# A long convolution's spectrum of half 0, stored with one frequency word per row instead of one signal per row

## The chip, the cores and the metric

The kernel runs on one core of a Trainium2 chip. The metric is the device time of one execution, in microseconds (us). Before the change the median of three runs is 1404.55 us (1404.37 to 1404.98). The core has five engines that matter here: PE (matrix multiplications, with the loading of weights counted apart as PEld), DVE and ACT (element-wise work, both read PSUM), POOL (element-wise work in SBUF) and SP, which issues most DMAs.

## The reference

The program is a long convolution, whose result goes through two expert layers. The convolution is the part that the change touches.

```python
def _attn_ref(x, v, pos_emb, w1, w2):          # S = 12480, D = 128
    h_mlp = np.maximum(pos_emb @ w1, 0.0) @ w2
    window = np.exp(-0.01 * np.arange(S))[:, None]
    h_filt = h_mlp * window
    u = x * v
    Uf = np.fft.rfft(u, n=2 * S, axis=1)
    Hf = np.fft.rfft(h_filt, n=2 * S, axis=0)
    y = np.fft.irfft(Uf * Hf[None], n=2 * S, axis=1)[:, :S, :]
    return x * y

def _moe_ref(x, w_in, w_out):    return np.maximum(x @ w_in, 0.0) ** 2 @ w_out
def _moe2_ref(x, w_in, w_out, alpha):
    h = x @ w_in
    return (np.maximum(h, 0.0) + alpha * np.minimum(h, 0.0)) @ w_out
```

## The kernel before

The transform of length L = 110 x 229 = 25190 is done by two small matrix transforms, over NA = 110 and over NB = 229 points, of which symmetry leaves HB = 115 rows and KA = 56 columns, as real and imaginary part K2 = 112 words. All of it is fp32 matmuls; each such matmul stands in the trace as two records of PE and two weight loads. The 128 signals (channels) are worked in two halves of 64, and each has an even and an odd part, so a half's spectrum is 115 partitions x 128 signal parts x 112 words.

Half 0's spectrum lies in gaps of the large tile `G`, which is looked at as HX = 116 rows of two blocks of 128 words (`gap`, L129): a row is one signal part, 112 adjacent words; the first XF = 16 rows are in block 0, the other 112 in block 1 (`U`, L131). Because of the two places, `parts(0)` (L138) names two ranges, of 16 and of 112 rows, and each operation on all of half 0 is issued once for each. Half 1's spectrum lies in one piece in `R2`. The other rows of block 0 serve as staging tiles for the loaded `x` and `v` (`xv_ring`, NV = 10 pairs) and for copies (`a_ring`, `t_ring`).

The work around the change is in stages, written as generators; `run` (L452) interleaves the steps of two of them in program order, by a fixed share. Each engine takes its own instructions in that order.

- `u_stage(0)` (L327) beside `r_stage` (L236): for 16 groups of four signals, `u_mm_a3` does the first transform (L283, L286, L287) and `u_mm_b3` the second (L296, ACT's copy L298, and DVE's sum and difference L301, which write half 0's spectrum). `r_stage` transforms the filter (L242, L244, L248, L249) and spills it. `prep` (POOL, L271 and L210) and `load` (SP, L263) run some groups ahead.
- `u_stage(1)` (L309 to L325, no split) beside `p_stage(0)` (L342): 14 steps n, each in two half steps of four matmuls (L368, the filter's values into a PSUM bank `H`), a DVE product of spectrum and filter (L373) into `T` or the PSUM tile `wide`, then two DVE operations (L382) and the closing sum and difference back into the spectrum (`finish`, L352, on POOL).
- `p_stage(1)`, called `q0`, beside `b_stage(0)` (L386), the inverse transform of half 0: three half steps of `q0` first, then 25 half steps beside 16 steps of `b_stage`. A step has 8 matmuls (L391), each with one signal part's 112 words as weights, and two ACT copies (L399).
- `b_stage(1)` with the decoding of expert weights, then `y_stage` (L444, L445), whose weights are words two apart, and then the two expert layers (L605 to L658), from about 340 us to the end.

Of the kernel before, what the change touches and what calls it, by code (L numbers as in the profile page):

```python
# [9 lines left out]
F32 = mybir.dt.float32  # L10
# [5 lines left out]
ALU = mybir.AluOpType  # L16

S, D, F, FF = 12480, 128, 64, 2048
# [3 lines left out]
KA = HA + 1  # L22
K2 = 2 * KA
HB = (NB + 1) // 2
# [1 line left out]
HX = 2 * HP  # L26
HZ = (HB + 1) // 2
KP = KA // 2
XF = 16
NAP = -(-NA // 16) * 16  # L30
DH = D // 2
DG = 4
NG = DH // DG
# [20 lines left out]
def ring_of(pool, n, shape, dtype, name):  # L54
    return Ring(pool.tile(shape, dtype, name=f"{name}{i}") for i in range(n))
# [3 lines left out]
def kernel(  # L59
# [22 lines left out]
    nc = tc.nc  # L82
# [16 lines left out]
    r_any, r_a, r_b, r_h = Ring(banks), Ring(banks[0:2]), Ring(banks[2:5]), Ring(banks[5:8])  # L99
    r_ab, r_y = Ring([]), Ring([])  # L100

    def bank(ring, p, *dims):
        n = 1
        for d in dims:
            n *= d
        names = "uvwxyz"[:len(dims)]
        return ring()[:p, :n].rearrange(
            f"p ({' '.join(names)}) -> p {' '.join(names)}", **dict(zip(names, dims))
        )
# [3 lines left out]
    R2 = p_r2.tile([128, K2 * 128], F32, name="R2")  # L113
# [8 lines left out]
    isinb, icosb = dfb[:, 1], dfb[:, 2]  # L122
# [5 lines left out]
    gv = G[:K2].rearrange("p (t e x r) -> p t e x r", t=HP, e=2, r=2)  # L128
    gap = [G.rearrange("p (n h x) -> p n h x", h=2, x=128)[:, :, h] for h in range(2)]  # L129

    def U(h, x0, n):  # L131
        if h:
            return R2[:HB].rearrange("p (x k) -> p x k", k=K2)[:, x0:x0 + n]
        if x0 < XF:
            return gap[0][:HB, x0:x0 + n, 128 - K2:128]
        return gap[1][:HB, x0 - XF:x0 - XF + n, 0:K2]

    def parts(h):  # L138
        return [(0, D)] if h else [(0, XF), (XF, D - XF)]

    NV = 10
    at = [XF]

    def rows(n):
        at[0] += n
        assert at[0] <= HX
        return gap[0][:, at[0] - n:at[0]]

    a_ring = [[rows(DG)[:, :, 0:K2] for _ in range(2)] for _ in range(2)]
    t_ring = [rows(DG)[:, :, 0:K2] if i else gap[1][:, D - XF:D - XF + DG, 0:K2] for i in range(2)]  # L150
    n_old = -(-(HP - at[0]) // DG)
    old = [rows(DG) for _ in range(n_old)]
    n_pos = -(-(GH + HZ * NA - 256 * at[0]) // (256 * DG))
# [2 lines left out]
    xv_ring = new + after + old  # L156
    assert len(xv_ring) == 2 * NV
    xv_ring = list(zip(xv_ring[::2], xv_ring[1::2]))
# [99 lines left out]
    def load(n):  # L258
        while loaded[0] <= min(n, 2 * NG - 1):
            k = loaded[0]  # L260
            assert ready[0] > k - NV
            for t, src in zip(xv_ring[k % NV], (xs, vs)):
# [3 lines left out]
    def prep(n):  # L266
        while ready[0] <= min(n, 2 * NG - 1):
            k = ready[0]
            assert loaded[0] > k
            x, v = (t[:NA, :, 0:HB] for t in xv_ring[k % NV])  # L270
            nc.gpsimd.tensor_tensor(out=v, in0=v, in1=x, op=ALU.mult)  # L271
            signed(nc.gpsimd, x, v, DG)
            ready[0] += 1
# [15 lines left out]
    def u_mm_b3(k):  # L289
        hi, lo = a_t.pop(k)  # L290
        ps = [bank(r_b, HB, 2, DG, KA) for _ in range(2)]
        t = t_ring[k % 2][:HB].rearrange("p d (c k) -> p c d k", c=2)
        for eo in (1, 0):
            th, tl = (tab[:, eo] for tab in df3)
            for i, (w, x) in enumerate(((th, lo), (tl, hi), (th, hi))):
                nc.tensor.matmul(ps[eo], lhsT=w, rhs=x[:, eo], start=i == 0, stop=i == 2)  # L296
            if eo:
                nc.scalar.copy(out=t, in_=ps[1])  # L298
        u = U(0, 2 * DG * k, 2 * DG).rearrange("p (d s) (c k) -> p s c d k", s=2, c=2)
        for s, op in enumerate((ALU.add, ALU.subtract)):  # L300
            nc.vector.tensor_tensor(out=u[:, s], in0=ps[0], in1=t, op=op)  # L301

    def u_mm_a(k):
        q, u = (t[:NA, :, 0:HB] for t in xv_ring[k % NV])
# [5 lines left out]
            nc.scalar.copy(out=a_t[k][s], in_=p)  # L310

    def u_mm_b(k):
        h, g = divmod(k, NG)
        a = a_t.pop(k)
        pe = bank(r_b, HB, DG, 2, KA)
        po = bank(r_b, HB, DG, 2, KA)
        nc.tensor.matmul(po[:, :, 0], lhsT=sinb, rhs=a[0][:, :, 1])
        nc.tensor.matmul(pe[:, :, 0], lhsT=cosb, rhs=a[0][:, :, 0])
        nc.tensor.matmul(po[:, :, 1], lhsT=sinb, rhs=a[1][:, :, 0])
        t = t_ring[k % 2][:HB].rearrange("p d (c k) -> p d c k", c=2)  # L320
        nc.scalar.copy(out=t, in_=po)
        nc.tensor.matmul(pe[:, :, 1], lhsT=cosb, rhs=a[1][:, :, 1])
        u = U(h, 2 * DG * g, 2 * DG).rearrange("p (d s) (c k) -> p d s c k", s=2, c=2)
        for s, op in enumerate((ALU.add, ALU.subtract)):
            nc.vector.tensor_tensor(out=u[:, :, s], in0=pe, in1=t, op=op)  # L325

    def u_stage(h, parts=None):  # L327
        for k in range(h * NG, (h + 1) * NG + 1):
            if k < (h + 1) * NG:
                prep(k + NV - 4)  # L330
                load(k + NV - 1)
                u_mm_a3(k, parts) if parts else u_mm_a(k)
                yield
            if k > h * NG:
                u_mm_b3(k - 1) if parts else u_mm_b(k - 1)
                yield
# [3 lines left out]
    p_order += [(j + nj - 6) % nj for j in range(nj)]  # L340

    def p_stage(h, t_ring, r_ring):  # L342
        def at_j(x0, m, j):
            return U(h, x0, m).rearrange("p x (c k) -> p x c k", c=2)[:, :, :, 4 * j:4 * j + 4]

        def finish(n, j, A):
            eng = nc.vector if n == 2 * nj - 1 else nc.gpsimd
            for x0, m in parts(h):
                y = A[:, x0:x0 + m].rearrange("p (d s) c k -> p d s c k", s=2)
                u = at_j(x0, m, j).rearrange("p (d s) c k -> p d s c k", s=2)  # L350
                for s, op in ((0, ALU.add), (1, ALU.subtract)):
                    eng.tensor_tensor(out=u[:, :, s], in0=y[:, :, 0], in1=y[:, :, 1], op=op)  # L352

        for n in range(h * nj, (h + 1) * nj):
            j = p_order[n]
            m = p_order[min(n + 2, 2 * nj - 1)]
            if m not in r_t:
                del r_t[p_order[n - 1]]
                r_t[m] = r_ring()
                nc.sync.dma_start(out=r_t[m].rearrange("p q c k -> p (q c k)"), in_=spill[m])  # L360
            r = r_t[j]
            A = t_ring()
            B = wide[:HB].rearrange("p (x c k) -> p x c k", k=4, c=2)
            for c, out_c in enumerate((A, B)):
                H = bank(r_h, HB, DH, 2, 2, 2)
                for q in range(2):
                    for s in range(2):
                        nc.tensor.matmul(  # L368
                            H[:, :, s, q], lhsT=r[:, q, 2 * s + c], rhs=w2_sb[:, h * D:(h + 1) * D]
                        )  # L370
                hv = H.rearrange("p d s q r -> p (d s) (q r)")
                for x0, m in parts(h):
                    nc.vector.tensor_tensor(  # L373
                        out=out_c[:, x0:x0 + m],
                        in0=at_j(x0, m, j),
                        in1=hv[:, x0:x0 + m].unsqueeze(2).to_broadcast([HB, m, 2, 4]),
                        op=ALU.mult,
                    )
                if c == 0:
                    yield  # L380
            for c, op in ((0, ALU.subtract), (1, ALU.add)):
                nc.vector.tensor_tensor(out=A[:, :, c], in0=A[:, :, c], in1=B[:, :, 1 - c], op=op)  # L382
            finish(n, j, A)
            yield

    def b_stage(h, alone):  # L386
        for g in range(NG):
            for e in range(2):
                p = bank(r_y if alone else r_ab, K2, DG, HX)
                for d in range(DG):  # L390
                    nc.tensor.matmul(  # L391
                        p[:, d], lhsT=U(h, 2 * (g * DG + d) + e, 1)[:, 0], rhs=icosb if e == 0 else isinb
                    )
                dst = gv[:, :, e, h * DH + g * DG:h * DH + (g + 1) * DG]
                src = p.rearrange("p d (t r) -> p t d r", r=2)
                if alone and e and g == NG - 1:
                    nc.vector.tensor_copy(out=dst, in_=src)
                else:
                    nc.scalar.copy(out=dst, in_=src)  # L399
            yield  # L400
# [171 lines left out]
    n = NCH * NT  # L572
    i = j = 0
# [143 lines left out]
    with tc.manual_schedule():  # L717
        with ExitStack() as st:
            late = st.enter_context(tc.tile_pool(name="late", bufs=1, side="right"))
            w2_sb = late.tile([128, 2 * D], F32, name="w2_sb")  # L720
# [23 lines left out]
            (wide,) = last_two("wide", 1024)  # L744
            r_b.items, r_h.items, r_ab.items = six[2:4], six[4:6], six[0:4]
            big = st.enter_context(tc.tile_pool(name="tt", bufs=1, side="right"))
            tt = ring_of(big, 2, [HB, D, 2, 4], F32, "T")
            p0, q0 = p_stage(0, tt, r_ring), p_stage(1, tt, r_ring)
            run((u_stage(1), 2 * NG), (p0, 2 * nj - 4))
            next(back)  # L750
# [13 lines left out]
        with tc.tile_pool(name="wo", bufs=1) as wo:  # L764
# [5 lines left out]
            for _ in ys:  # L770
                n = min(left, 4)
# [159 lines left out]
```

## Time and profile before

| | us |
|---|---|
| median of three runs | 1404.55 |
| the profiled execution's own time | 1402.77 |
| its span, first to last instruction | 1401.0 |
| PE / PEld busy | 1389.3 / 1205.7 |
| DVE / ACT / POOL busy | 1158.4 / 977.8 / 1006.9 |

The numbers of the trace come from the profiled execution; its own time is 1.8 us below the median. Busy time counts an engine as busy while any of its instructions is under way. PE's records overlap one another (the next begins while the last one drains), so PE looks busy even where it is not at its peak; the distance from one record's start to the next tells its pace. Idle time of an engine that sets nothing costs nothing.

### The profile page before, as it was taken

How to read it: one execution, taken by the hardware profiler on the slowest of the kernel's cores; microseconds unless marked ns; L12 is line 12 of the kernel's file. 1: busy time of each engine (PE TensorE's matmuls, PEld its weight loads, DVE VectorE, ACT ScalarE, POOL GpSimd, SP SyncE). 2: the span in 40 equal slices, each digit the busy share in tenths (PEclk: the TensorE clock that was granted, in tenths of full speed). 3: DMA queues.
4: the chain of work that ended last, by engine and by line, in shares of the span. 5: the costliest groups of instructions: out<-in, count | busy, mean ns of one | idle time of the engine just before them, and what ended most of it. 6: DMA issues, size and time to landing. Idle time of an engine off the chain costs nothing.

```text
span 1401.0 us, 22648 instructions
## 1 busy us (share of the span) xinstructions
PE 1389.3 (99%) x7566; PEld 1205.7 (86%) x7566; DVE 1158.4 (83%) x1824; ACT 977.8 (70%) x1850; POOL 1006.9 (72%) x841
## 2 busy tenths in 40 slices
PE   9999999999999999999999999999999999999998
PEld 9999989998888888888888888888888888888898
DVE  5688899786888888888888888788888878888888
ACT  4454322725988778778777877877787787777777
POOL 4954856446787777877777777777777777777777
PEclk9999999999999999999999999999999999999999
DMA  7565323397000000000000000000000000000000
GB/s 209 173 200 177 94 82 109 105 275 218 24 16 1 8 1 9 8 8 8 9 8 0 9 8 9 8 8 8 8 2 8 8 9 8 9 8 1 8 9 19
DMA packets 59016, 66.20 MB, mean 47 GB/s; under 512 B 6226, under 2 KB 48019, under 8 KB 58771
## 3 DMA queue, kind: packets, MB, share of 16 engines
q1 hardware_dynamic: 57802, 60.62, 14.3%
q0 software_dynamic: 688, 3.93, 0.8%
q8 instruction: 59, 0.97, 0.3%
q14 instruction: 58, 0.48, 0.1%
q10 hardware_dynamic: 409, 0.21, 0.1%
HBM read 47.83 MB, written 16.92 MB: 46 GB/s over the span
## 4 chain that ended last, share of the span: by engine, by line
PE 79%; ACT 1%; POOL 1%; DVE 1%; issue 0%; POOLq 0%; DVEq 0%
PE bank L605 19%; PE bank L607 19%; PE bank L606 19%; PE pair L606 6%; PE pair L607 6%; PE pair L605 6%; PE bank L444 2%; PE bank L445 2%; ACT G L399 1%; POOL g L658 1%; ACT pair L517 0%; ACT w_i L487 0%; DVE pair L477 0%; DVE f_w L481 0%; DVE pair L475 0%
## 5 line engine op out<-in xcount | busy, mean ns | idle before, releaser
L658 POOL TENSOR_TENSOR g<-R,g 128x512 fp32r<-128x512 f32 (+1 forms) x601 | 779.4, 1314 | 253.5 <-ACT g L647 241.3
L640 DVE SCALAR_TENSOR_TENSOR R<-bank,e 128x512 f32<-128x512 f32 (+1 forms) x800 | 530.1, 672 | 137.4 <-POOL g L658 99.8
L647 ACT CAST g<-R 128x512 fp32r<-128x512 f32 (+1 forms) x800 | 469.8, 605 | 77.5 <-DVE R L640 70.0
L625 ACT ACTIVATE e<-bank 128x512 f32<-128x512 f32 (+1 forms) x400 | 235.0, 587 | 106.6 <-PE bank L607 104.6
L630 DVE TENSOR_SCALAR e<-bank,alpha 128x512 f32<-128x512 f32 (+1 forms) x266 | 195.0, 733 | 36.0 <-PE bank L607 34.4
L658 DVE TENSOR_TENSOR g<-R,g 128x512 fp32r<-128x512 f32 (+1 forms) x199 | 184.7, 928 | 0.0
L606 PE MATMUL pair<-g,w_o 128*128 128x512 f32 (+1 forms) x400 | 153.7, 384 | 0.4 <-POOL g L658 0.4
L605 PE MATMUL bank<-x,w_i 128*128 128x512 f32 (+1 forms) x400 | 153.8, 384 | 0.0
L605 PE MATMUL pair<-g,w_o 128*128 128x512 f32 (+1 forms) x400 | 153.6, 384 | 0.0
L606 PE MATMUL bank<-x,w_i 128*128 128x512 f32 (+1 forms) x400 | 153.6, 384 | 0.0
L607 PE MATMUL bank<-x,w_i 128*128 128x512 f32 (+1 forms) x400 | 153.5, 384 | 0.0
L607 PE MATMUL pair<-g,w_o 128*128 128x512 f32 (+1 forms) x400 | 153.5, 384 | 0.0
L605 PE MATMUL bank<-g,w_o0b 128*128 128x512 f32 (+1 forms) x350 | 134.4, 384 | 0.0
L606 PE MATMUL bank<-g,w_o0b 128*128 128x512 f32 (+1 forms) x350 | 134.3, 384 | 0.0
L607 PE MATMUL bank<-g,w_o0b 128*128 128x512 f32 (+1 forms) x350 | 134.3, 384 | 0.0
L627 ACT ACTIVATE e<-bank 128x512 f32<-128x512 f32 (+1 forms) x134 | 78.7, 588 | 33.5 <-PE bank L607 32.9
L628 ACT ACTIVATE e<-e,alpha 128x512 f32<-128x512 f32 (+1 forms) x134 | 95.5, 713 | 4.4
L605 PEld LDWEIGHTS bank<-x,w_i 128*128 128x128 f32 x400 | 75.1, 188 | 15.0 <-DVE R L640 0.9
L606 PEld LDWEIGHTS pair<-g,w_o 128*128 128x128 f32 x400 | 75.2, 188 | 14.8 <-POOL g L658 1.0
L607 PEld LDWEIGHTS bank<-x,w_i 128*128 128x128 f32 x400 | 75.1, 188 | 14.4
L607 PEld LDWEIGHTS pair<-g,w_o 128*128 128x128 f32 x400 | 75.1, 188 | 14.4
L606 PEld LDWEIGHTS bank<-x,w_i 128*128 128x128 f32 x400 | 75.2, 188 | 13.8
(137 smaller groups left out, 2526.0 us busy)
## 6 DMA issues: line engine op xcount, KB each, us to landing
r<-spill SPq DMA_DIRECT2D x22, 460.0 KB, 3.2
G<-in_xs_dram SPq DMA_DIRECT2D x32, 224.0 KB, 3.5
G<-in_vs_dram SPq DMA_DIRECT2D x32, 224.0 KB, 3.5
spill<-r SPq DMA_DIRECT2D x14, 460.0 KB, 3.0
out_dram<-R SPq DMA_DIRECT2D x23, 256.0 KB, 2.0
R<-in_xt_dram SPq DMA_DIRECT2D x27, 218.0 KB, 4.2
s_w<-in_moe_w_in_dram SPq DMA_DIRECT2D x16, 256.0 KB, 3.6
s_w<-in_moe_w_out_dram SPq DMA_DIRECT2D x16, 256.0 KB, 2.7
```

Source lines behind the costliest of these rows:

```text
L444: nc.tensor.matmul(pv, lhsT=le, rhs=re, start=True, stop=False)
L445: nc.tensor.matmul(pv, lhsT=lo, rhs=ro, start=False, stop=True)
L605: nc.tensor.matmul(p, lhsT=wl, rhs=xh, start=first, stop=False)
L606: nc.tensor.matmul(p, lhsT=wh, rhs=xl, start=False, stop=False)
L607: nc.tensor.matmul(p, lhsT=wh, rhs=xh, start=False, stop=last)
L625: nc.scalar.activation(out=r, in_=p, func=ACTF.Relu)
L627: nc.scalar.activation(out=r, in_=p, func=ACTF.Relu, scale=-1.0)
L628: nc.scalar.activation(out=r, in_=r, func=ACTF.Copy, scale=alpha[:, t:t + 1])
L630: nc.vector.tensor_scalar(out=r, in0=p, scalar1=0.0, scalar2=alpha[:, t:t + 1], op0=ALU.min, op1=ALU.mult)
L640: nc.vector.scalar_tensor_tensor(out=g, in0=p, scalar=0.0, in1=r, op0=ALU.max, op1=op)
L647: nc.scalar.copy(out=gh, in_=g)
L658: eng.tensor_tensor(out=gl, in0=g, in1=gh.bitcast(F32), op=ALU.subtract)
```

## The change

Half 0's spectrum moves to block 1 of `G` alone, as 112 rows, one per word (c, k) of the spectrum, each with its 128 signal parts side by side, ordered (s, d): s is even or odd part, d the signal. Rows are 256 words apart. `u_cells` gives the weights of one signal part for `b_stage`. `T`, `wide` and the PSUM bank `H` take the same order for half 0 and keep the old one for half 1. `parts` and with it the second instruction of each pair go away. The 16 rows of block 0 that become free are four more staging tiles: two more pairs, NV = 12.

```diff
-    def U(h, x0, n):
-        if h:
-            return R2[:HB].rearrange("p (x k) -> p x k", k=K2)[:, x0:x0 + n]
-        if x0 < XF:
-            return gap[0][:HB, x0:x0 + n, 128 - K2:128]
-        return gap[1][:HB, x0 - XF:x0 - XF + n, 0:K2]
-
-    def parts(h):
-        return [(0, D)] if h else [(0, XF), (XF, D - XF)]
-
-    NV = 10
-    at = [XF]
+    u0 = gap[1][:HB, :K2].rearrange("p (c k) (s d) -> p c k s d", c=2, s=2)
+    u1 = R2[:HB].rearrange("p (d s c k) -> p d s c k", s=2, c=2, k=KA)
+
+    def u_cells(h, d, e):
+        if h:
+            return u1[:, d, e].rearrange("p c k -> p (c k)")
+        return gap[1][:HB, :K2, e * DH + d]
+
+    NV = 12
+    at = [0]
...
     def u_mm_b3(k):
...
-        u = U(0, 2 * DG * k, 2 * DG).rearrange("p (d s) (c k) -> p s c d k", s=2, c=2)
         for s, op in enumerate((ALU.add, ALU.subtract)):
-            nc.vector.tensor_tensor(out=u[:, s], in0=ps[0], in1=t, op=op)
+            u = u0[:, :, :, s, DG * k:DG * (k + 1)].rearrange("p c k d -> p c d k")
+            nc.vector.tensor_tensor(out=u, in0=ps[0], in1=t, op=op)
...
     def u_stage(h, parts=None):
         for k in range(h * NG, (h + 1) * NG + 1):
             if k < (h + 1) * NG:
-                prep(k + NV - 4)
+                prep(k + NV - 6)
                 load(k + NV - 1)
...
     def p_stage(h, t_ring, r_ring):
+        def shaped(t):
+            if h:
+                return t.rearrange("p (d s c k) -> p c (d s) k", s=2, c=2, k=4)
+            return t.rearrange("p (c k x) -> p c k x", c=2, k=4)
+
+        def at_j(j):
+            k = slice(4 * j, 4 * j + 4)
+            if h:
+                return u1[:, :, :, :, k].rearrange("p d s c k -> p c (d s) k")
+            return u0[:, :, k].rearrange("p c k s d -> p c k (s d)")
...
         def finish(n, j, A):
             eng = nc.vector if n == 2 * nj - 1 else nc.gpsimd
-            for x0, m in parts(h):
-                y = A[:, x0:x0 + m].rearrange("p (d s) c k -> p d s c k", s=2)
-                u = at_j(x0, m, j).rearrange("p (d s) c k -> p d s c k", s=2)
-                for s, op in ((0, ALU.add), (1, ALU.subtract)):
-                    eng.tensor_tensor(out=u[:, :, s], in0=y[:, :, 0], in1=y[:, :, 1], op=op)
+            if h:
+                y, u = A.rearrange("p (d s z) -> p s d z", s=2, z=8), u1[:, :, :, :, 4 * j:4 * j + 4]
+                u = [u[:, :, s] for s in range(2)]
+            else:
+                y = A.rearrange("p (z s d) -> p s z d", s=2, z=8)
+                u = [u0[:, :, 4 * j:4 * j + 4, s] for s in range(2)]
+            for s, op in ((0, ALU.add), (1, ALU.subtract)):
+                eng.tensor_tensor(out=u[s], in0=y[:, 0], in1=y[:, 1], op=op)
...
             for c, out_c in enumerate((A, B)):
-                H = bank(r_h, HB, DH, 2, 2, 2)
+                H = r_h()[:HB].rearrange("p (d s q r) -> p s q d r" if h else "p (q r s d) -> p s q d r", s=2, q=2, r=2)
                 for q in range(2):
                     for s in range(2):
-                        nc.tensor.matmul(
-                            H[:, :, s, q], lhsT=r[:, q, 2 * s + c], rhs=w2_sb[:, h * D:(h + 1) * D]
-                        )
-                hv = H.rearrange("p d s q r -> p (d s) (q r)")
-                for x0, m in parts(h):
-                    nc.vector.tensor_tensor(
-                        out=out_c[:, x0:x0 + m],
-                        in0=at_j(x0, m, j),
-                        in1=hv[:, x0:x0 + m].unsqueeze(2).to_broadcast([HB, m, 2, 4]),
-                        op=ALU.mult,
-                    )
+                        nc.tensor.matmul(H[:, s, q], lhsT=r[:, q, 2 * s + c], rhs=w2_sb[:, h * D:(h + 1) * D])
+                hv = H.rearrange("p s q d r -> p (d s) (q r)" if h else "p s q d r -> p (q r) (s d)")
+                o, u = shaped(out_c), at_j(j)
+                if h:
+                    o, u = (x.rearrange("p c x k -> p x c k") for x in (o, u))
+                    hv = hv.unsqueeze(2).to_broadcast([HB, D, 2, 4])
+                else:
+                    hv = hv.unsqueeze(1).to_broadcast([HB, 2, 4, D])
+                nc.vector.tensor_tensor(out=o, in0=u, in1=hv, op=ALU.mult)
...
     def b_stage(h, alone):
...
-                        p[:, d], lhsT=U(h, 2 * (g * DG + d) + e, 1)[:, 0], rhs=icosb if e == 0 else isinb
+                        p[:, d], lhsT=u_cells(h, g * DG + d, e), rhs=icosb if e == 0 else isinb
```

## Rows read from the trace of the kernel before

**Rows 1.** Busy time by stage; columns: stretch, length, engines (x instructions), clock, DMA.
```profile
core 0: us, PE busy (x) PEld busy (x) DVE busy (x) ACT busy (x) POOL busy (x), PEclk, DMA share, GB/s
45.00:116.60 71.60, 71.16 (x586) 68.60 (x585) 58.45 (x122) 35.58 (x77) 44.79 (x39) 1.00 0.64 194
116.60:195.00 78.40, 75.25 (x601) 72.87 (x600) 69.17 (x115) 25.45 (x48) 53.03 (x67) 0.98 0.38 117
...
200.60:250.70 50.10, 49.12 (x451) 47.02 (x450) 48.37 (x55) 16.90 (x31) 32.29 (x26) 1.00 0.35 103
250.70:276.40 25.70, 25.64 (x259) 25.45 (x257) 20.83 (x51) 20.64 (x52) 13.36 (x19) 1.00 0.32 94
```
**Rows 2.** Who waited for whom, 45 to 116.6 us.
```profile
engine line waited for: us in total, times, longest us
POOL G L271 <- DMA G<-in_vs_dram: 15.8, 8, 3.8
...
DVE xl L287 <- ACT xh L286: 6.7, 31, 0.4
...
DVE G L301 <- PE bank L296: 2.8, 10, 0.9
...
PEld bank L296 <- DVE G L301: 0.6, 1, 0.6
```
**Rows 3.** Who waited for whom, 116.6 to 195 us, and 195 to 250.7 us.
```profile
DVE wide L373 <- PE bank L368: 3.6, 4, 1.2
...
DVE T L373 <- PE bank L368: 1.3, 1, 1.3
...
PEld bank L368 <- DVE T L373: 3.3, 11, 0.5
```
**Rows 4.** PE: one group by line, then instructions in order of time (start, length).
```profile
L391 PE MATMUL bank<-dfb,R 115*112 115x116 f32 x256 | 25.5, 263 | 0.0
...
81.28 1.04 PE L242 MATMUL pair<-dfb,R 115*128 115x115 f32 x8
...
82.16 1.77 PE L283 MATMUL bank<-dfa,G 110*115 110x112 f32 x16
...
125.96 1.04 PE L368 MATMUL bank<-w_sb,r 128*115 128x128 f32 x8
...
126.83 1.77 PE L309 MATMUL bank<-dfa,G 110*115 110x112 f32 x16
...
289.83 0.40 PE L445 MATMUL bank<-ido,G 112*128 112x110 f32 x2
...
295.95 0.28 PE L445 MATMUL bank<-ido,G 112*128 112x110 f32 x1
...
699.77 0.39 PE L605 MATMUL pair<-g,w_o 128*128 128x512 f32 x1
...
703.17 0.39 PE L605 MATMUL bank<-x,w_i 128*128 128x512 f32 x1
```
**Rows 5.** DVE by line and shape, 0 to 340 us; columns: busy us, mean ns.
```profile
L301 DVE TENSOR_TENSOR G<-bank,G 115x448 f32<-115x448 f32 x32 | 18.5, 619 | 3.6 <-PE bank L296 2.8 <-ACT G L298 0.5
...
L197 DVE SCALAR_TENSOR_TENSOR G<-bank,win_sb 110x512 f32<-110x512 f32 x7 | 7.4, 1058 | 6.3 <-PE bank L190 6.3
...
L197 DVE SCALAR_TENSOR_TENSOR G<-bank,win_sb 110x256 f32<-110x256 f32 x1 | 0.6, 602 | 0.0
```
**Rows 6.** DVE's products in order of time: half 0's pairs, then half 1's.
```profile
127.42 1.42 DVE L373 TENSOR_TENSOR wide<-G,bank 115x128 f32<-115x128 f32 x2
...
130.07 1.28 DVE L373 TENSOR_TENSOR T<-G,bank 115x128 f32<-115x128 f32 x2
...
197.08 1.21 DVE L373 TENSOR_TENSOR T<-R,bank 115x1024 f32<-115x1024 f32 x1
...
198.36 1.23 DVE L373 TENSOR_TENSOR wide<-R,bank 115x1024 f32<-115x1024 f32 x1
```
**Rows 7.** The closing operations by line and shape, 0 to 340 us.
```profile
L382 DVE TENSOR_TENSOR T<-T,wide 115x512 f32<-115x512 f32 x56 | 36.0, 683 | 1.0
...
L352 POOL TENSOR_TENSOR R<-T 115x512 f32<-115x512 f32 x26 | 32.3, 1264 | 15.5 <-DVE T L382 15.5
L352 POOL TENSOR_TENSOR G<-T 115x448 f32<-115x448 f32 x28 | 31.1, 1132 | 0.0
...
L352 POOL TENSOR_TENSOR G<-T 115x64 f32<-115x64 f32 x28 | 8.4, 320 | 33.8 <-DVE T L382 33.7
```

More of the change, by code (lines that the diff above doesn't have):

```diff
@@ L28 @@
 KP = KA // 2
-XF = 16
 NAP = -(-NA // 16) * 16
@@ L149 @@
     a_ring = [[rows(DG)[:, :, 0:K2] for _ in range(2)] for _ in range(2)]
-    t_ring = [rows(DG)[:, :, 0:K2] if i else gap[1][:, D - XF:D - XF + DG, 0:K2] for i in range(2)]
+    t_ring = [rows(DG)[:, :, 0:K2] if i else gap[1][:, K2:K2 + DG, 0:K2] for i in range(2)]
     n_old = -(-(HP - at[0]) // DG)
@@ L312, in u_mm_b @@
     def u_mm_b(k):
-        h, g = divmod(k, NG)
+        g = k - NG
         a = a_t.pop(k)
@@ L322, in u_mm_b @@
         nc.tensor.matmul(pe[:, :, 1], lhsT=cosb, rhs=a[1][:, :, 1])
-        u = U(h, 2 * DG * g, 2 * DG).rearrange("p (d s) (c k) -> p d s c k", s=2, c=2)
         for s, op in enumerate((ALU.add, ALU.subtract)):
-            nc.vector.tensor_tensor(out=u[:, :, s], in0=pe, in1=t, op=op)
+            nc.vector.tensor_tensor(out=u1[:, DG * g:DG * (g + 1), s], in0=pe, in1=t, op=op)
     def u_stage(h, parts=None):
@@ L342, in p_stage @@
     def p_stage(h, t_ring, r_ring):
-        def at_j(x0, m, j):
-            return U(h, x0, m).rearrange("p x (c k) -> p x c k", c=2)[:, :, :, 4 * j:4 * j + 4]
+        def shaped(t):
[7 more added lines that the diff above has]
+            return u0[:, :, k].rearrange("p c k s d -> p c k (s d)")
         def finish(n, j, A):
             eng = nc.vector if n == 2 * nj - 1 else nc.gpsimd
-            for x0, m in parts(h):
-                y = A[:, x0:x0 + m].rearrange("p (d s) c k -> p d s c k", s=2)
-                u = at_j(x0, m, j).rearrange("p (d s) c k -> p d s c k", s=2)
-                for s, op in ((0, ALU.add), (1, ALU.subtract)):
-                    eng.tensor_tensor(out=u[:, :, s], in0=y[:, :, 0], in1=y[:, :, 1], op=op)
+            if h:
[6 more added lines that the diff above has]
+                eng.tensor_tensor(out=u[s], in0=y[:, 0], in1=y[:, 1], op=op)
         for n in range(h * nj, (h + 1) * nj):
@@ L362, in p_stage @@
             A = t_ring()
-            B = wide[:HB].rearrange("p (x c k) -> p x c k", k=4, c=2)
+            B = wide[:HB]
             for c, out_c in enumerate((A, B)):
-                H = bank(r_h, HB, DH, 2, 2, 2)
+                H = r_h()[:HB].rearrange("p (d s q r) -> p s q d r" if h else "p (q r s d) -> p s q d r", s=2, q=2, r=2)
                 for q in range(2):
                     for s in range(2):
-                        nc.tensor.matmul(
-                            H[:, :, s, q], lhsT=r[:, q, 2 * s + c], rhs=w2_sb[:, h * D:(h + 1) * D]
-                        )
-                hv = H.rearrange("p d s q r -> p (d s) (q r)")
-                for x0, m in parts(h):
-                    nc.vector.tensor_tensor(
-                        out=out_c[:, x0:x0 + m],
-                        in0=at_j(x0, m, j),
-                        in1=hv[:, x0:x0 + m].unsqueeze(2).to_broadcast([HB, m, 2, 4]),
-                        op=ALU.mult,
-                    )
+                        nc.tensor.matmul(H[:, s, q], lhsT=r[:, q, 2 * s + c], rhs=w2_sb[:, h * D:(h + 1) * D])
[7 more added lines that the diff above has]
+                nc.vector.tensor_tensor(out=o, in0=u, in1=hv, op=ALU.mult)
                 if c == 0:
                     yield
+            a, b = shaped(A), shaped(B)
             for c, op in ((0, ALU.subtract), (1, ALU.add)):
-                nc.vector.tensor_tensor(out=A[:, :, c], in0=A[:, :, c], in1=B[:, :, 1 - c], op=op)
+                nc.vector.tensor_tensor(out=a[:, c], in0=a[:, c], in1=b[:, 1 - c], op=op)
             finish(n, j, A)
@@ L746 @@
             big = st.enter_context(tc.tile_pool(name="tt", bufs=1, side="right"))
-            tt = ring_of(big, 2, [HB, D, 2, 4], F32, "T")
+            tt = ring_of(big, 2, [HB, D * 8], F32, "T")
             p0, q0 = p_stage(0, tt, r_ring), p_stage(1, tt, r_ring)
```

## The prediction

> **What bounds the kernel now.** I read the busy time by stage first. The spectrum work has four stages around the change: A, signals of half 0 with the filter's first transforms (45 to 116.6 us); B, signals of half 1 beside the products of half 0 (to about 200 us); C, products of half 1 beside the inverse transform of half 0, `b_stage(0)` (200.6 to 250.7 us); D, `b_stage(1)` [rows 1]. PE is covered in nearly all of A, B and C, but that is overlap of records, so the next view is who waited for whom. In A, PE's waits for DVE come to 0.6 us while DVE waits 6.7 and 2.8 us [rows 2]: PE sets A, and DVE's 58.45 us leave 13.15 us free [rows 1]. In B, DVE waits 3.6 + 1.3 us for PE's products [rows 3]; PE is covered 75.25 of 78.40 us, DVE 69.17 [rows 1]: PE sets most of B, and DVE the tail in which only `p0` is left. In C, PE's weight loads wait 3.3 us, 11 times, for a DVE product [rows 3] and DVE is busy 48.37 of 50.10 us [rows 1]: DVE sets C, with PE close behind.
>
> How close is a sum. A record of `b_stage` comes every 25.5 us / 256 = 99.6 ns, one of the filter's product matmul (L368) every (126.83 - 125.96) / 8 = 109 ns [rows 4]. From 200.6 us on, PE has 256 records of `b_stage(0)` and 25 of the 28 half steps of `q0` left (3 are taken ahead), of 8 records each: 256 x 99.6 = 25.5 us and 200 x 109 = 21.8 us, together 47.3 of 50.1 us. So 2.8 us of slack, or 11 ns per record of `b_stage(0)`, keep PE from setting C.
>
> **The change, part by part.** Half 0's spectrum was 128 rows, one per signal, of 112 adjacent words; it becomes 112 rows, one per frequency word, of 128 adjacent signals, with rows 256 words (1 KB) apart. Four places touch it.
>
> *1. Writes of `u_mm_b3` (L301), stage A.* The order of elements stays c, d, k with k innermost, and k now steps 1 KB: every element lands alone. Now 448 elements take 619 ns [rows 5]. The nearest row with such a write is L197, whose innermost output step is 230 words: 1058 ns for 512 elements, 602 for 256 [rows 5], so 456 / 256 = 1.78 ns per element and 146 ns fixed. L301 then takes 146 + 448 x 1.78 = 943 ns: +324 ns x 32 = +10.4 us of DVE. The cover is DVE's 13.15 us of idle in A. It doesn't all fit: 58.45 + 10.4 = 68.9 of 71.6 us, 96% of an engine whose work comes in bursts behind ACT copies. Ends: 0 (hidden) and +10.4 us (exposed). I take +2.5, nearer to hidden, because the idle is larger than the addition. A gain is excluded, since nothing gets shorter.
>
> *2. Products and closing operations of half 0 (L373, L352, L382), stage B.* Out go 28 of 56 DVE products and 28 of 56 POOL operations; elements stay the same, and DVE's and POOL's runs become longer, 64 or 128 instead of 4. Half 1 already has the unparted form: its product for T takes 1.21 us where half 0's pair takes 1.28, and for wide 1.23 against 1.42 [rows 6]. So 0.07 + 0.19 = 0.26 us per step, x14 = -3.6 us of DVE. As PE sets most of B, most of it is idle time given back: I take -1.5 us (ends 0 and -3.6). POOL loses 2 x (1132 + 320) - 2 x 1264 = 376 ns per step [rows 7]; only the last step's is on the path, as `b_stage(0)` begins behind it: -0.3 us. L382 keeps its 512 elements; at 683 ns [rows 7] less 146 they cost 1.05 ns each already in runs of four, against 1.78 for lone words, so longer runs have little to give: nothing.
>
> *3. The product matmul's writes to PSUM (L368, half 0), stage B.* It wrote pairs of adjacent words (r innermost); it now writes single words, r stepping 128 words. No row shows such a write. Low end 0: such a record has 0.85 ns per column (109 / 128), while the expert layers' records write 512 adjacent words in (703.17 - 699.77) / 15 = 227 ns, 0.44 ns each [rows 4], so a lone word has the time in which there two pass. High end, a write rate halved: 224 records x 109 = +24 us on PE, which sets B. I take 0 and keep the other as a rival.
>
> *4. Weight loads of `b_stage(0)` (L391), stage C.* `u_cells` for half 0 is one signal's column: 112 words, each 1 KB from the last, where now they are adjacent. Weight loads run beside the matmul before, so what counts is the larger of the two. That loads are no small party the rows show: with 128 weight columns and 115 moving, L242 has a record every (82.16 - 81.28) / 8 = 110 ns, against 99.6 ns for L391 with 112 and 116 [rows 4]; the spacing grows with the weights, about 0.86 to 0.89 ns per weight column. So any slowing of the load is passed on at once. Low end: L444 and L445 load 128 weights two words apart, two records in 0.235 us (26 groups of two from 289.83 to 295.95) = 118 ns, 8 over L242 [rows 4]; that would make 7 ns here, inside C's slack: 0. High end: the 1.78 ns per lone element of L197: 112 x 1.78 = 199 ns per record, twice as long as now. The step of 1 KB is that row's kind (230 words) and not the two-word one, in which half of the words still have a neighbour close by; I take 199 ns. PE from 200.6 us: 256 x 199 + 21.8 = 50.9 + 21.8 = 72.7 us, in place of 50.1: **+22.6 us**. Late then is PE's queue: `q0`'s matmuls wait behind loads, DVE idles some 24 us of C, POOL behind it, and D can't begin before PE is through with `b_stage(0)`. Nothing gives it back: D is the same work on the adjacent layout of half 1.
>
> The Trainium skill has the same rule for the memory: *SBUF — State Buffer* (Door 1: The DMA port swizzle) says that accesses keep full bandwidth while at least two fall into one 16-byte line, and pay for each new line beyond; it names no figure for weight loads. L444's two-word step (two hits per line, +8 ns) agrees; no run here shows the lone word on PE. *Vector Engine (DVE) Microarchitecture Reference* (5.2, Measured stream behaviour) has 1.71 to 1.76 ns per hopping element; an estimate from it is 192 to 197 ns per record, C +21 to +22 us.
>
> *5. Four more staging tiles.* NV goes from 10 to 12, loads run 11 steps ahead instead of 9, `prep` stays 6 ahead. The first call in A issues 4 more DMAs on SP, in front of the first spill of `r`; the last calls in B issue none. `r`'s ring of three gives that spill some ten us. POOL's waits for these loads are 15.8 us in A [rows 2]; some of them go, but nothing waited for POOL there, so nothing moves: 0.
>
> **The sum.** A +2.5, B -1.5 - 0.3, C +22.6: +23.3 us on the profiled execution's 1402.77 us (span 1401.0), 1426.1. The median of the runs shown is 1404.55, 1.8 above it: 1427.9, I say 1427.5. All that follows at 340 us is untouched.
>
> **The rivals.**
> *Loads are fetched without a price for the hop* (then C stays on DVE, 0). For: L444 pays only 8 ns for a hop of two words. Against: both engines' rows with a lone word at a distance. Then +2.5 - 1.8 = +0.7: 1405.3, no change.
> *The other side: faster.* Loads are free as above, DVE's idle time in A takes all 10.4 us, and B falls by DVE's whole 3.6 us and POOL's 0.3, if PE's waits in B were behind DVE after all: -3.9 us, 1400.7. It decides from where A's exposed part is under 1 us and `b_stage(0)`'s record stays under 110 ns. Against it: DVE waits for PE in B [rows 3].
> *Lone PSUM words cost a second slot.* L368 of half 0 comes every 218 ns, and B grows by up to 24 us of PE: 1404.55 + 2.5 + 23 = 1430 with C unchanged, 1450 with C as in my sum. For it: nothing in the profile but the missing row; against it: the half-used rate in part 3. *PSUM — Partial Sum Buffer* in the Trainium skill (Specifications) says that PSUM lines are 8 bytes and that a non-contiguous pattern slows matmuls significantly. By it the pairs of words were fit and the lone words are not; no row of before can tell.
> *A alone is exposed*: DVE sets A, +5 to +10: 1408 to 1413.
>
> **How the numbers follow.** Forecast (weight loads bound C, +13 to +28 us, by 165 to 220 ns per record) 0.57; PSUM words too, or instead, 0.09; A exposed without C 0.07; no change 0.16; faster 0.11. Within 0.2% (2.8 us) is what a measurement of this kernel can't tell from no change. Slower is 0.57 + 0.09 + 0.07 = 0.73, same 0.16, faster 0.11. The likeliest case alone spans 1417 to 1433; the range goes down to 1403, to hold the no-change case, and up to 1434; left out are the faster case and most of the PSUM one.
>
> **What would show it.** Records of L391 from G about 199 ns apart and their weight loads longer than 177 ns; C some 72 us long with DVE idle for a third of it, waiting for L368; D unchanged. L301 at 0.94 us, and PE's waits for DVE in A above 0.6 us. 28 products of half 0 at about 1.22 us. L368 still 109 ns apart in B. The forecast is wrong if L391 stays near 100 ns apart, or if C's end isn't PE's.

## The result and the profile after

The changed kernel takes 1423.02 us (median of 4 runs, 1422.75 to 1424.36), the kernel before 1404.46 us: a ratio of 1.0137, 95% interval 1.0124 to 1.0150. It is slower by 18.6 us, by 20.4 us in the profiled spans (1421.4 against 1401.0). The forecast was 1427.5 us.

The span is the profiled execution's time from its first to its last instruction. The stages again, now cut at the first PE record of each, first the kernel before, then the changed one. Columns as in [rows 1]; A, B, C and D from top to bottom.

```profile
44.56:115.46 70.90, 70.46 (x578) 67.91 (x577) 57.81 (x120) 35.54 (x77) 45.23 (x39) 1.00 0.64 192
115.46:200.68 85.22, 82.05 (x642) 79.34 (x641) 75.58 (x122) 25.71 (x49) 56.95 (x72) 0.96 0.38 117
200.68:250.79 50.11, 49.13 (x451) 47.03 (x450) 48.29 (x55) 16.93 (x31) 32.29 (x26) 1.00 0.35 103
250.79:277.72 26.93, 25.55 (x258) 25.36 (x256) 21.46 (x51) 21.87 (x53) 14.58 (x20) 1.00 0.34 101
```
```profile
45.49:116.91 71.42, 70.46 (x578) 67.90 (x577) 62.89 (x120) 35.52 (x77) 45.10 (x39) 1.00 0.64 191
116.91:201.16 84.25, 79.84 (x642) 76.98 (x640) 73.19 (x94) 25.71 (x49) 53.32 (x44) 1.00 0.36 107
201.16:271.24 70.08, 70.08 (x450) 70.08 (x449) 49.00 (x55) 16.94 (x31) 32.41 (x26) 1.00 0.25 73
271.24:298.20 26.96, 25.58 (x258) 25.40 (x257) 21.46 (x51) 21.86 (x53) 14.59 (x20) 1.00 0.35 100
```

A is 0.52 us longer, B 0.97 shorter, C 19.97 longer, D the same. From D's start to the end it is 1150.2 us in both spans; in the profiles of four runs below it is 1151.8, with the same work, so a whole run's time moves by over a microsecond without the change. A begins 0.93 us later (45.49 for 44.56), which as far as the runs show isn't the change: those below begin it anywhere from 44.56 to 45.49, late with the old layout (45.35 in *Lone weights alone*) and early with the new one (44.71 in *Runs of four*).

Not all of B's 0.97 us is the change. The clock that TensorE was granted in B is 0.96 in the profile before: 1.00 (2.4 GHz) from 187 to 192 us, and 0.50 (1.2 GHz) from 193 to 199, behind a wait of PE for DVE of 1.77 us. Three runs below do in B what the kernel before does, with a clock of 1.00, and all three take 84.99 us; this is the row of *Lone weights alone*:

```profile
116.25:201.24 84.99, 79.84 (x641) 76.97 (x640) 75.45 (x122) 25.68 (x49) 56.92 (x72) 1.00 0.39 117
```

So at the same clock B is 84.99 before and 84.25 after: the change saves 0.74 us there, and 0.23 us are the clock.

In C, PE and its weight loads are now busy without a gap, while DVE has the same 49 us of work in 70. The changed kernel's instructions by line, in the order of [rows 4], [rows 5] and [rows 7] (L397 was L391, L375 was L368, L298 was L301, L383 was L373, L388 was L382, L359 was L352):

```profile
L397 PE MATMUL bank<-dfb,G 115*112 115x116 f32 x256 | 51.4, 355 | 0.0
L397 PEld LDWEIGHTS bank<-dfb,G 115*112 115x112 f32 x256 | 50.3, 285 | 0.0
...
L359 POOL TENSOR_TENSOR G<-T 115x512 f32<-115x512 f32 x28 | 35.1, 1274 | 43.4 <-DVE T L388 42.5 <-DMA r<-spill 0.8
...
L298 DVE TENSOR_TENSOR G<-bank,G 115x448 f32<-115x448 f32 x32 | 27.8, 946 | 3.5 <-PE bank L293 2.7 <-ACT G L295 0.5
L397 PE MATMUL bank<-dfb,R 115*112 115x116 f32 x256 | 25.6, 263 | 0.0
L397 PEld LDWEIGHTS bank<-dfb,R 115*112 115x112 f32 x256 | 25.5, 177 | 0.0
...
L383 DVE TENSOR_TENSOR wide<-G,bank 115x1024 f32<-115x1024 f32 x14 | 17.1, 1223 | 3.8 <-PE bank L375 3.8
...
L383 DVE TENSOR_TENSOR T<-G,bank 115x1024 f32<-115x1024 f32 x14 | 17.0, 1212 | 0.7 <-PE bank L375 0.7
```

The same line L397 costs 51.4 us with weights from `G` (lone words) and 25.6 with weights from `R2` (adjacent); its weight loads take 285 ns, against 177 for adjacent ones. PE in C in order of time, start and length:

```profile
233.97 3.24 PE L397 MATMUL bank<-dfb,G 115*112 115x116 f32 x16
237.04 1.91 PE L375 MATMUL bank<-w_sb,r 128*115 128x128 f32 x16
238.79 1.50 PE L397 MATMUL bank<-dfb,G 115*112 115x116 f32 x7
```

A step of `b_stage(0)` has 16 records in 3.07 us, 192 ns each (99.6 before). The two half steps of `q0` behind it take 1.75 us, 109 ns each, as before. Who waits for whom in C:

```profile
POOL R L359 <- DVE T L388: 29.7, 13, 4.2
DVE wide L383 <- PE bank L375: 15.1, 12, 2.6
```

DVE's product waits for PE now, 12 times; before, PE's weight loads waited for DVE [rows 3].

### The profile page after: what moved, and what is told of

Read it like the earlier page. It is cut to its first block, busy times and chain, and to the rows that moved or that the text cites. A ratio compares the mean times of both kernels' runs of the same rounds, so it can differ in the third digit from the quotient of the medians.

```text
span 1421.4 us, 22581 instructions
## 1 busy us (share of the span) xinstructions
PE 1409.0 (99%) x7566; PEld 1227.6 (86%) x7566; DVE 1162.5 (82%) x1796; ACT 978.1 (69%) x1850; POOL 1003.3 (71%) x813
## 3 DMA queue, kind: packets, MB, share of 16 engines
q0 software_dynamic: 688, 3.93, 0.8%
## 4 chain that ended last, share of the span: by engine, by line
PE 78%; ACT 1%; POOL 1%; DVE 1%; issue 0%; POOLq 0%; DVEq 0%
PE bank L611 19%; PE bank L612 19%; PE bank L613 19%; PE pair L612 6%; PE pair L611 6%; PE pair L613 6%; PE bank L450 2%; PE bank L451 2%; ACT G L405 1%; POOL g L664 1%; ACT pair L523 0%; ACT w_i L493 0%; DVE pair L483 0%; DVE f_w L487 0%; DVE pair L481 0%
```

## The experiments

Stage lengths below are cut as above, in the profile of each run.

**Adjacent weights in the changed kernel.** The edit:

```diff
-        return gap[1][:HB, :K2, e * DH + d]
+        return gap[1][:HB, (2 * d + e) % K2, :K2]
```

> The changed kernel, but b_stage(0) loads its weights from 112 adjacent words of a row of the spectrum's place (wrong values; all else as changed). Theory: the loss is the price of lone words in weight loads, about 94 ns on each of 256 records of stage C. Then those records come every 99 to 100 ns again, C falls from 70 to 50 us, and the time to 1403 us (20 below the changed kernel, 1 to 2 below the kernel before, as B's 1 us is kept). Rival: C is long because of the order of its work or of its PSUM banks, and the load only looks long because it waits: the time stays at 1423 us.

Measured: 1403.6 us, ratio to before 0.9998 (0.9988 to 1.0007). A 71.42, B 84.24, C 50.12 us. C's busy row and its PE group, in the run's own profile:

```profile
201.11:251.23 50.12, 49.20 (x451) 47.03 (x450) 48.37 (x55) 16.91 (x31) 32.30 (x26) 1.00 0.35 102
```
```profile
L397 PE MATMUL bank<-dfb,G 115*112 115x116 f32 x256 | 27.7, 262 | 0.0
```

The whole loss is gone with the lone words of the weights, with everything else of the change in place. The rival, that C is long by the order of its work or of its PSUM banks, falls: both are as in the changed kernel. Of the forecast gain of 1 to 2 us the times show nothing that clears the interval. The stages say why: at the same clock B is 0.75 us shorter than with the old layout, but A is 0.52 longer, which leaves about 0.2.

**Lone weights alone in the kernel before.** The edit:

```diff
-                        p[:, d], lhsT=U(h, 2 * (g * DG + d) + e, 1)[:, 0], rhs=...
+                        p[:, d], lhsT=U(h, 2 * (g * DG + d) + e, 1)[:, 0] if h else gap[1][:HB, :K2, (2 * (g * DG + d) + e) % K2],
```

> The kernel before, with one edit: b_stage(0) takes its weights as 112 words 256 words apart from the block in which half 0 lies (wrong values; no new layout, no merged operations, no staging tiles). Theory: this alone makes the loss: records of b_stage(0) every 193 ns, C 70 us, time 1404.5 + 20 = 1424 to 1425 us. Rival: the loss needs the other parts of the change too (DVE's hop writes, lone PSUM words, staging): under 1410 us.

Measured: 1423.18 us, ratio 1.0137 (1.0122 to 1.0152), the changed kernel's own. C:

```profile
201.24:271.22 69.98, 69.98 (x451) 69.98 (x450) 48.98 (x55) 16.95 (x31) 32.46 (x26) 1.00 0.25 73
```

One operand's step, in a kernel that is otherwise the one before, makes the loss; A (70.90 us) and B (84.99) don't have it.

**Runs of four in A.** The halves are ordered c, k, d, so DVE writes four adjacent words per row:

```diff
-            src = p.rearrange("p d c k -> p c d k")
+            src = p.rearrange("p d c k -> p c k d")
...
-        ps = [bank(r_b, HB, 2, DG, KA) for _ in range(2)]
+        ps = [bank(r_b, HB, 2, KA, DG) for _ in range(2)]
...
-            u = u0[:, :, :, s, DG * k:DG * (k + 1)].rearrange("p c k d -> p c d k")
+            u = gap[1][:HB, :K2, x0:x0 + DG].rearrange("p (z y) d -> p z y d", z=4)
```

> The changed kernel, with the halves of stage A ordered so that DVE writes half 0's spectrum in runs of four adjacent words instead of lone ones; nothing left out. Theory: DVE's operation falls from 946 to about 620 ns, 10.4 us less DVE in A, but PE sets A, so the time falls by 0.5 us at most: 1422.5 us. Rival: A's exposed part is larger than the trace lets see, because the deeper staging gives something back at the same place: 1420 us or less.

Measured: 1423.16 us, which can't be told from 1423.02. In its profile the operation takes 620 ns and A 70.91 us, 0.51 less than in the changed kernel and 0.01 more than before. So the 0.52 us that A grew are the lone writes, all of it, and the rest of DVE's longer records was hidden.

**Loads nine steps ahead.**

```diff
-                load(k + NV - 1)
+                load(k + NV - 3)
```

> The changed kernel with its 12 pairs of staging tiles, but loads issued 9 steps ahead, as before, instead of 11. Theory: nothing waits for POOL's preparation, so the longer lead gave nothing: 1423 us, within 1. Rival: the lead took back 1 to 2 us of A: 1424 to 1425 us.

Measured: 1423.5 us (1422.51 to 1424.31); A 71.42, B 84.24, C 70.09 us, each the changed kernel's. POOL's waits for the loads in A are 17.1 us (8 times) with this lead and 11.0 us (5 times) with the longer one; no stage is longer for it.

**Which steps cost.** In the kernel before, `b_stage(1)` gets another weight step in each of its 16 groups:

```diff
+STEP = [1, 2, 3, 4, 5, 6, 8, 12, 16, 24, 32, 64, 72, 112, 127, 128]
...
+    def cells(g):
+        return R2[:HB, 0:K2 * STEP[g]].rearrange("p (n w) -> p n w", w=STEP[g])[:, :, 0]
...
+                        p[:, d], lhsT=cells(g) if h else U(h, 2 * (g * DG + d) + e, 1)[:, 0], rhs=icosb if e == 0 else isinb
```

> The kernel before, with b_stage(1) (stage D) loading its 112 weights from words 1, 2, 3, 4, 5, 6, 8, 12, 16, 24, 32, 64, 72, 112, 127 and 128 apart, one step for each of its 16 groups (wrong values). Theory: a weight pays for every step to a new piece of 16 bytes, so step 1 gives 99 to 100 ns per record, step 2 about 105, step 3 about 150, and every step of 4 and more about 193. Rival: the price hangs on the distance (rows of 1 KB fall into the same bank): 193 at 128 but less at small or odd steps; or as DVE does by the Trainium skill, more at 24.

It was executed once. The weight loads (L395 here) of nine groups in order of time, for steps of 1, 2, 3, 4, 12, 16, 24, 72 and 128 words (mean ns of one in the last column before the bar):

```profile
L395 PEld LDWEIGHTS bank<-dfb,R 115*112 115x112 f32 x15 | 1.6, 177 | 0.0
L395 PEld LDWEIGHTS bank<-dfb,R 115*112 115x112 f32 x15 | 1.6, 182 | 0.0
L395 PEld LDWEIGHTS bank<-dfb,R 115*112 115x112 f32 x15 | 2.4, 241 | 0.0
L395 PEld LDWEIGHTS bank<-dfb,R 115*112 115x112 f32 x15 | 3.2, 303 | 0.0
L395 PEld LDWEIGHTS bank<-dfb,R 115*112 115x112 f32 x16 | 3.8, 336 | 0.0
L395 PEld LDWEIGHTS bank<-dfb,R 115*112 115x112 f32 x16 | 3.2, 286 | 0.0
L395 PEld LDWEIGHTS bank<-dfb,R 115*112 115x112 f32 x16 | 3.6, 319 | 0.0
L395 PEld LDWEIGHTS bank<-dfb,R 115*112 115x112 f32 x16 | 3.4, 306 | 0.0
L395 PEld LDWEIGHTS bank<-dfb,R 115*112 115x112 f32 x16 | 3.2, 285 | 0.0
```

The median distance from one record to the next, in ns:

| step, words | 1 | 2 | 3 | 4 | 5, 6 | 8, 72 | 12 | 24 | 127 | 16, 32, 64, 112, 128 |
|---|---|---|---|---|---|---|---|---|---|---|
| ns | 99 | 104 | 153 | 207 | 194, 195 | 209 | 233 | 220 | 202 | 191 to 192 |

Steps of two words are nearly free, steps of three cost some 60% of the full addition, and from four on a weight costs 1.71 to 2.08 ns, near or far. So it isn't the 1 KB: the rival of one bank falls, since 5 words cost as much as 128 (194 and 192 ns). The theory's numbers hold at 1, 2, 3, 5, 6 and at multiples of 16; that 4, 8, 12, 24 and 72 cost more than 16 it did not foresee. The second rival, more at 24, has the sign right there (220), but 12 words cost more still (233). Why stays open.

**Weights gathered by ACT.** To keep the new layout and load adjacent weights, on top of runs of four:

```diff
+    def gather(i):
+        if i < 2 * NG:
+            g, e = divmod(i, 2)
+            x0 = e * DH + g * DG
+            cells[i] = w_ring()
+            nc.scalar.copy(out=cells[i], in_=gap[1][:HB, :K2, x0:x0 + DG].rearrange("p k d -> p d k"))
...
+                        lhsT=u_cells(h, g * DG + d, e) if h else cells[2 * g + e][:, d],
```

> The changed kernel with runs of four in A, and with ACT gathering the four columns of each step of b_stage(0) into adjacent words one step ahead (two buffers), so that PE loads adjacent weights; nothing left out. [...] Theory (PE's weight loads alone made C long): PE falls back under DVE, C is 50 to 53 us, the time 1403 to 1406 us. Rival: ACT's gathers with two buffers become C's bound, C 60 us or more, 1413 us.

Measured: 1407.31 us, ratio 1.0023 (1.0013 to 1.0033); C 53.58 us. Most of the loss is gone, but not all: the kernel stays 0.2% slower than the one before. The rest is at C's end, where DVE and `q0` are nearly done and only ACT's chain stands (L400 is the gather, L412 the matmul of `b_stage`, L422 ACT's copy of its result):

```profile
248.90 1.05 PE L412 MATMUL bank<-dfb,G 115*112 115x116 f32 x8 [0.27 <-ACT G L400]
...
249.16 1.02 ACT L400 COPY tabs<-G 115x448 f32<-115x448 f32 x1
250.04 0.58 ACT L422 COPY G<-bank 112x464 f32<-112x464 f32 x1
250.23 0.87 PEld L412 LDWEIGHTS bank<-dfb,tabs 115*112 115x112 f32 x8 [0.46 <-ACT tabs L400]
250.23 1.05 PE L412 MATMUL bank<-dfb,tabs 115*112 115x116 f32 x8 [0.28 <-ACT tabs L400]
250.47 1.01 ACT L400 COPY G<-G 115x448 f32<-115x448 f32 x1
```

Eight records come every 1.30 to 1.33 us there, set by a gather of 1.02 us and the copy behind it; eight records of adjacent weights take 0.8 us of PE [rows 4].

**Lone weights in a quarter.** As in the second experiment, with `if h or g % 4` for `if h`.

> The kernel before with lone weight words in every fourth group of b_stage(0), 64 of 256 records (wrong values). Theory: PE has 2.8 us of slack against DVE in C; 64 x 94 ns = 6.0 us more on PE leave 3.2 us: C 53.3 us. Rival: each lone load delays C by its full price, there is no slack to use up: C 55 to 56 us (a quarter of 20 us and more).

Measured: 1409.22 us, in a single execution; C 55.99 us (the row ends 0.04 us before it):

```profile
201.24:257.20 55.96, 54.30 (x450) 52.71 (x449) 48.55 (x55) 16.95 (x31) 32.27 (x26) 1.00 0.31 92
```

C grew by 5.9 us, and 64 records at 192 - 99.6 ns are 5.9 us. The rival was right: a few slow groups pay in full, 1.5 us each. The starts of the steps in the two traces show where. The first and the 13th step have only one half step of `q0` beside them; PE waits for nothing in them, before or here, and each grows from 2.46 us to 3.93 and 3.94. The fifth and the ninth have two half steps; they grow from 3.77 and 3.78 us to 4.81 and 4.80, that is by 1.03, and the step behind each by another 0.44, from 3.59 to 4.03. In that step PE now waits for DVE's product:

```profile
220.94 1.75 PE L391 MATMUL bank<-dfb,G 115*112 115x116 f32 x16
222.53 1.04 PE L368 MATMUL bank<-w_sb,r 128*115 128x128 f32 x8
224.00 1.13 PE L368 MATMUL bank<-w_sb,r 128*115 128x128 f32 x8 [0.43 <-DVE T L373]
```

So what these two steps take from PE's slack comes back as a wait in the step behind.

**Gathers split between ACT and POOL.**

```diff
-            nc.scalar.copy(out=cells[i], ...)
+            copy = nc.gpsimd.tensor_copy if i % 4 == 3 or i >= 26 and i % 2 else nc.scalar.copy
+            copy(out=cells[i], ...)
```

> The kernel with gathered weights, with ten of its 32 gathers given to POOL (every fourth, and the odd ones of the last three steps); nothing left out. In the kernel with ACT alone C took 53.6 us; ACT's gathers of 1.02 us and its copies of 0.55 us make 50.2 us and stand alone in the last three steps. Theory: ACT was that rest, with 40 us it isn't any more, C falls to DVE's 50.1 to 50.5 us, and with A as before and B 1 us shorter the profiled stages add up to 0.5 to 1 us below the kernel before; the measured time 1403 to 1404.5 us, hardly told from before. Rival: POOL's gathers hold up its closing operations, on which DVE's next product waits: C 53 us or more, 1406 us or more.

The edit gives POOL nine gathers, not the ten that the expectation names. Measured: 1443.16 us, ratio 1.0281 (1.0267 to 1.0295); C 91.35 us. The rival's engine was right, its size far too small. One turn in order of time (L401 is the gather, L413 the matmul of `b_stage`, L378 the filter's product matmul, L386 DVE's product, L391 the two DVE operations behind it, L362 the closing operations):

```profile
216.12 1.28 DVE L391 TENSOR_TENSOR T<-T,wide 115x512 f32<-115x512 f32 x2
...
217.48 2.47 POOL L362 TENSOR_TENSOR R<-T 115x512 f32<-115x512 f32 x2 [1.65 <-DVE T L391]
219.88 0.94 POOL L401 COPY tabs<-G 115x448 f32<-115x448 f32 x1
...
220.87 1.89 PE L413 MATMUL bank<-dfb,tabs 115*112 115x116 f32 x8 [4.39 <-POOL tabs L401]
...
222.56 3.52 PE L378 MATMUL bank<-w_sb,r 128*115 128x128 f32 x16
...
224.51 1.23 DVE L386 TENSOR_TENSOR wide<-R,bank 115x1024 f32<-115x1024 f32 x1 [5.98 <-PE bank L378]
```

The gather stands on POOL behind the closing operations, these wait for DVE, DVE's next product waits for PE, and PE waits for the gather: four engines in a ring, one at a time, nine times for 28.0 us of PE. After such a wait of 4.39 us PE's 16 records take 3.52 us instead of 1.91. The granted clock is 0.50 (1.2 GHz) from 220.8 to 222.5 us, where PE starts again, and 1.00 (2.4 GHz) from 226 to 230, where it has worked on; over the whole of C it is 0.78. So the ring costs its waits and, beside them, slower records.

No version tried here that keeps the result right beats the kernel before.

## Why the prediction was right

The mechanism forecast as likeliest is the one that made the loss: shown by taking the lone weights away (C 50.12 us) and by adding them alone (C 69.98 us). The stated range, from no change up to 1434 us, is wide enough to say little by itself; it is the steps that bear the forecast out:

| step | predicted, us | measured, us |
|---|---|---|
| A, lone writes of DVE | +2.5 | +0.52 |
| B, merged operations, lone PSUM words | -1.8 | -0.97 (-0.74 at the same clock) |
| C, lone weight words | +22.6 | +19.97 |
| staging tiles | 0 | 0 |
| D and all behind it | 0 | 0.0 |
| A's later start | not in the sum | +0.93 |
| span | +23.3 | +20.4 |

*1, A.* The operation was forecast at 943 ns and takes 946. The share that shows was mis-sized, 2.5 for 0.52 us. It comes in PE's one wait for DVE, at A's end:

```profile
PEld bank L293 <- DVE G L298: 1.1, 1, 1.1
```

It was 0.6 us before [rows 2]. The sum of 10.4 us was too large as well, since a record's length is not what it holds DVE for. In the changed kernel's DVE stream

```profile
82.47 1.73 DVE L298 TENSOR_TENSOR G<-bank,G 115x448 f32<-115x448 f32 x2
84.05 0.38 DVE L245 TENSOR_TENSOR r<-pair,rt 128x230 f32<-128x230 f32 x1
```

the pair's records end at 84.20, and the next instruction has begun at 84.05. DVE's busy time in A rose by 5.1 us (57.81 to 62.89), not by 10.4, with 13.1 us of idle time to take it.

*2, B.* The pairs did become 1212 and 1223 ns, as half 1's. With PE setting most of B, 0.74 of the 1.8 us came through; that PE's clock was not full in the rows of B (0.98 in [rows 1]) the prediction passed over.

*3, PSUM.* L375 of half 0 writes lone words and comes every 109 ns as before: the low end was right, and the rival of a second slot falls for these records. *PSUM — Partial Sum Buffer* of the Trainium skill (Specifications), by which a non-contiguous pattern slows matmuls significantly, doesn't show in these fp32 records; at 0.44 ns per column, the rate of the expert layers, no run here tried it.

*4, C.* The term was too large by 2.6 us, for two reasons. A record takes 191.8 ns in the mean, not 199 (1.8 us over 256): 1.71 ns per lone word instead of L197's 1.78. And `q0` had 192 records left at C's start, not 200 (0.9 us): `run` takes a fourth half step before the first step of `b_stage(0)`, so that 24 and not 25 half steps stand beside it, which the working missed. With both, 256 x 191.8 + 192 x 109.3 ns = 49.1 + 21.0 = 70.1 us, the measured C. That the spacing grows with the weights is half of what [rows 4] show: L368, with 115 weight columns and 128 moving ones, comes every 109 ns as well, so the larger count sets it. In `b_stage`, with 112 and 116, the two are close, and a dearer load shows at once, by 5 ns at a step of two words. *SBUF — State Buffer* of the Trainium skill (Door 1: The DMA port swizzle), by which two accesses in one 16-byte line go at full rate and each new line costs, agrees with steps of 1, 2 and 16 words here (99, 104, 192 ns); of the higher price at 4, 8, 12, 24 and 72 words it says nothing.

*5, staging.* The longer lead, undone, moved no stage by more than 0.01 us.

The slack was read wrongly in two respects. With 192 records of `q0` it is 50.1 - 25.4 - 21.0 = 3.7 us and not 2.8. And as a sum over the stage it holds when every group is slow, but it is not there to be drawn on by a few: it stands in the steps that have two half steps of `q0` beside them, and in the first, the 13th and the last three steps PE waited for nothing and had none to give.

## What to carry to other kernels

A layout is chosen for all who read it: here it spared DVE and POOL 28 instructions each, worth 0.7 us, and nearly doubled the spacing of 256 records (99.6 to 191.8 ns), because their weight columns are about as many as the moving ones, so that the matmul beside a load was too short to hide a longer one. Before a tensor is turned, list each reader and writer with its innermost step, and look for one whose engine is within a few per cent of setting its stage. And a copy that is to repair it belongs on an engine whose queue doesn't wait, through others, for the consumer of that copy.

## What the runs showed that was not expected

- A weight load's price per step isn't even: 12 words apart 233 ns per record, 24 apart 220, 16 or 128 apart 192.
- ACT's gather of 448 words, read one by one 256 words apart and written side by side, takes 1017 ns, and POOL's the same in 989: POOL, at 1264 ns for 512 words of a sum [rows 7], is not behind ACT here.
- Stages repeat far better than whole runs: C is 70.08, 70.09 and 70.09 us in three kernels whose medians spread over half a us, so a change of 0.5 us that no median shows can be read from a stage, once the granted clock of the two stages has been compared: in B it alone made 0.2 us.
